# DeltaNet and MLP mixer on one core: the same steps in another global issue order

## The chip, the cores and the metric

The kernel runs on one core of one Trainium2 chip. Its time is the time on the device of one launch, in microseconds (us). The shares and durations come from a profile of one execution: TensorE is PE in it (its weight loads PEld), VectorE is DVE, ScalarE is ACT, GpSimd is POOL, and SyncE is SP, whose queue issues all the DMAs here.

## The reference, cut to what matters

```
# q, k, v: 4 batches x 8 heads x 768 steps x 48; beta: one weight per step
k_n = k / (norm(k) + 1e-6)
for t in range(768):                       # per batch and head, state is 48 x 48
    y[t] = q[t] @ state
    v_old = state.T @ k_n[t]
    state = state + beta[t] * outer(k_n[t], v[t] - v_old)
x = y, heads side by side                  # 4 x 768 x 384
h = relu(x.T @ w_tok1) @ w_tok2            # mixes the 768 tokens, through 256
u = x + h.T
out = u + relu(u @ w_ch1) @ w_ch2          # mixes the 384 channels, through 1536
```

All of it is computed in fp32. The MLP's weights arrive as 64-bit floats and are turned into fp32 words on the core.

## The kernel before

The recurrence is worked in chunks. A unit `u` is 128 steps of all 8 heads of one batch (24 units), and one recurrence step `t` is half a unit, 64 steps of the sequence (48 of them). Within a unit the dependence between its steps is a triangular matrix that is inverted; between units a 48 x 48 state is carried. The whole program is written as small jobs, each a Python generator that issues a few instructions and yields:

- `k{u}` (`load_kq`) loads k and q of a unit. From unit 12 on, the rows of k come first (calls 1 to 4, L363), then k in another arrangement, called kst (calls 5 to 8, L407), then the rows of q (calls 9 to 12, L363). `v{u}` (`load_v`) loads v in four DMAs (L407) and scales it on POOL (L416).
- `p{u}` (`prep`) squares kst on ACT (`ksq`, L442), makes the norms (L445 to L456), turns k and q (on PE, L466 and L484, for the first 12 units; with a transpose on DVE, L372, afterwards), multiplies them on PE (`p_g`, L504), masks on DVE (L510), and hands the blocks on: by copies (L569) for the first 6 units, by DMAs to DRAM (L577) for the others.
- `i{r}` (`invert`) inverts the triangles of a round of units on DVE (L613 to L641, in the main `sub` and `x`, L621 and L626). Rounds hold units 0-3, 4-5, 6-9, 10-13, and so on.
- `f{u}` (`from_parts`) brings the inverse back, by copies (L588) or DMAs (L593, `gm<-w_dram`); `h{u}` (`join_16`, L656 to L671) and `j{u}` (`join`, L685 to L718) complete the triangles from smaller ones.
- `r{t}` (`recur`) is the recurrence. PE computes `p_k` (L741), DVE `rest` (L746), PE `p_y` and `p_w` (L759, L763), ACT copies `w_t` (L767), PE computes `p_s` and the rest of `p_y` (L775, L776), DVE updates the state `s_t` (L785), ACT writes the result into `xb` (L790). The next step needs `s_t`.
- `m{b}` (`mixer`) is the MLP of batch b: token mixing (`p` L931, `p_h` L944), transposes (`p_ut` L954, copied to `u_t` L958), the first channel weight (batch 0: `p_c` L1011; the others: `p_r` L903, a scheme with 15 products of summed weights in place of 18), and the second (`p_o` L1033, seven products in place of eight). Its first six calls take one unit of the batch each as the recurrence writes it.
- `w{n}` turn the weights: a DMA (L271), two operations on ACT (L277, L278), one on DVE (L280), one on POOL (L285), one on DVE (L287). `s` (`sum_weights`) makes the sums of the first channel weight in 16 calls, one or two operations on DVE each (L842, L844). Six of these write into `lent`, the place of the k and q buffers of units up to 11, which have no other use afterwards; others overwrite blocks of the weight.
- `z`, `x` and `Y` (`keep_warm`, L225, and `warm_tiles`, L235) are fillers: matmuls of zeros into a PSUM tile that nobody reads.

No scheduler orders these at run time. A text at the end, `order`, names the job of which the next call is made, 2317 words with repeats (`p4*2` is two calls). All instructions are issued in that order; each engine, and SP's queue, executes its own in the order of issue, and waits for operands and buffers by semaphores:

```
for word in order.split():
    name, _, n = word.partition("*")
    for _ in range(int(n or 1)):
        next(jobs[name])
```

So the text decides for each engine what stands behind what. PSUM tiles come from four small sets: "prep" (2), "seq" (2, the recurrence), "mlp" (3) and the fillers' one.

Of the kernel before, what the change touches and what calls it, by code (L numbers as in the profile page):

```python
# [23 lines left out]
def kernel(  # L24
# [50 lines left out]
    NCB = DM // 128  # L75
# [182 lines left out]
    def piece_of(w, j, col):  # L258
        assert (id(w), j, col - col % WP) in rounded
        return w[:, j]  # L260
# [550 lines left out]
    }  # L811

    def sum_weights():
        for cb in range(NCB):
            for f in range(NHT):
                piece_of(wc1, cb, f * 128)
        a = {(j, k): w_block(j, k) for j in range(3) for k in range(NCB)}
        add, sub = ALU.add, ALU.subtract
        made = (
            ("w12", a[1, 2], a[0, 2], sub), ("w11", a[0, 1], "w12", add),  # L820
# [9 lines left out]
        for i, (out, x, y, op) in enumerate(made):  # L830
            j = {"w13": 0, "w9": 0, "w1": 0, "w6": 1, "w7": 2, "w15": 2}.get(out)
            assert j is None or used.issuperset(range(FT * j, FT * j + FT))
            outs = sums[out]
            n = WB // len(outs)
            for h, o in enumerate(outs):
                cut = slice(h * n, h * n + n)
                p, q = (
                    sums[z][0][:, cut] if isinstance(z, str) else z if z is None else z[:, cut]
                    for z in (x, y)
                )  # L840
                if p is None:
                    nc.vector.tensor_scalar_mul(o, q, -1.0)  # L842
                else:
                    nc.vector.tensor_tensor(out=o, in0=p, in1=q, op=op)  # L844
            if out not in [m[0] for m in made[i + 1 :]]:
                summed.add(out)
            yield
# [255 lines left out]
    jobs["z"] = keep_warm(4)  # L1103
    jobs["y"] = jobs["Y"] = warm_tiles()
    order = """
    z w10*5 b k1 k0 b k1*5 p1 k0*2 p1 w1 k0*3 p0*2 b p1 z p0*7 p1*2 k3 w1 w2 w1*2 p0 w3
    k2 k3 p0*2 w1 p0 p1 k2 w6 k3*2 p1 w2 k5 w3 p1*4 w2 w3 k2*2 k4*5 k2*2 p2 p1*2 w3
    k3*2 p0 p2 p3 p2 k4 p3 p2*4 w3 x p2*3 k6 p1 p3 p0*2 p2 p1 p2 v0 p2 w2 p1 w2 k5*4 p0
    p3*7 k7*5 z p4*2 w18 p1 p3*2 p2 p3 p2 z p4*2 p2 p3 p2 p3*2 w13 p3 p4*2 i0 k7 w18 p4
    i0*2 k6*4 k8 i0*3 v1*2 i0*7 p4*2 Y p4*2 w13 p4 i0 w13 i0 w18 z w18 i0 h0 p4 w6 p5*2  # L1110
    p4 i0 h1 w18 p5 h1 p6 k8*2 v0*3 f0*3 w13 f0 k8 w13 h0 w6 p6 h2 p5 h2 f1*3 k5 v1*2
    h0*2 p5 f1 h0 f2 h0*2 j0 k8 p5 w17 w6 z p5*2 p7 w8 f2 w17 k6 p6 w6 j0 h1 w17 w8 p7
    w17 z j0*2 h1 f2*2 h1 p4 j0 p6 w8*2 p4 h1*2 v0 p4 z w17 h2 r0 h2 r0 p5*2 r0 w14
    h2*3 w11 j1 w8 r0 Y w14*2 p5 v1 w11 Y p5 r1 k9 p5 r0 w11 j1*2 p5*2 h3 r1 p5 z j2 p6
    f3 r1*3 w14 w9 f3 h3 k8 p6 k9*4 p5 k9 i1 v2 j1 r1 z i1*2 w14 w9 i1 p6 r2*2 p8 v2 j1
    i1 w0 j2 i1*2 r1 i1 f3*2 r2 h3 r2*3 j2 p6 r3 w9 k10 h3*4 p6 w11*2 p6*2 r2 w0 r3*3
    w9 j3 v2*2 i1 w9 p7 w0 p6*2 w0 w5 r3 k10 j2*2 v2 r3 k10 r4 r3 v3 j3*2 p7*2 w0 p7
    w24 p7 k10*2 p6 p8*2 v3 r4 v3*2 p6 r4 j3 r4 p7 w16 j3 i1*2 p6 i1 p6 i1 r4 p7 r4*2
    w5 i1*2 p9 k11 p7 r5*2 w5*2 p7*2 r5*2 v4 p7*4 p9 r5*2 p7 w24 p8 r5 r6 w5 v3 r6 p9
    w16 p8*2 r6 i1 p8 h4*2 w16*2 h5 r6 h5 i1 p8*2 v4 w27 v4 r6 w16 r6*2 p8*2 f4*4 w27  # L1120
    w28 w24*2 p8*2 r7*2 k11 h4 v4 h4*4 w27 w24 w26 r7*2 w27*2 p8 p9*6 r7 w28 r7*2 w28
    w7 p9*2 p8 p9*2 p8*2 j4 p10 w28 j4 f5 w26 w28 f5 m0 f5*2 h5 x p9*4 w7 v4 w7*2 w29
    w7 j4 i2 h5 j4 h5 w26 w29 h5 w26*2 j4 v5 r8 w29*2 p10 r8 w15 h5 k12 r8 j5 r8 w15
    v5*3 w29 i2*3 w15*2 r8 j5 i2 w12 j5 v5 r8 r9 i2*2 k10 k11 m0 r8 r9*2 i2 w4 w15 i2
    w12 k11 k12*2 r9 k12 i2 r9 i2*3 w12 k11 i2 r9 w4 i2 r9 w4 m0 i2 w4 r10*2 j5 w12 w22
    p10*2 k12 p10 i2 w22 v6 m0 w4 j5 r10 i2 k12*6 w12 k12 r10*2 i2 r10*2 m0 r11 i2 w19
    i2 w22 z w22 w19*3 k11 w31 r11 p10 i2 v6 w22 i2 w21 w19 v6 r11 i2*5 v7 i2*2 v7*2 v6
    v7 p11 v6 i2 r11 i2 p10*4 w25 v7 r11 p10 r11 m0 w31 m0*2 f6*2 m0*2 f6 p11*2 p10
    f7*3 m0*2 w31*2 p10 w21 w31 m0*3 w25*3 f6 j6 f7 w21 p12 m0 j6*2 j7 m0 p12 w25*2 w23
    p12 f8 p12 w27 w25 j7*2 w27 w29 m0 f8*2 w20 p11*2 w21*2 w23*3 r12*2 p11 m0 j8 r12*2  # L1130
    p10*3 w20 r12 w23 w32 f9 w23 p10 j8*2 r13 f8 r13 w25 f9 w30 p11 m0 p11 p12 r13
    w20*2 r13*3 p11*2 f9 p11 k13*8 r14 w32 r13 w32*2 f9 p11*5 w20 p12*3 k13*2 p11 w32
    r14 k13 w30 w29 m0*4 r14*2 p12 v8*2 w30 k13 p12 r14 p13*3 w30 r14 w30 m0*2 w33
    p12*2 r15*2 v8 p13*3 w29 r14 m0*2 v8 r15 p13 r15 w33*2 m0*3 r15 k14*5 r15 p13 j9 v8
    p13*3 r16 w33*3 m0 w23 r16 k14*2 w33 m0 k14 r15 p12 w27 p12 w31 j9*2 p12 m0*2 r16*2
    p13*2 r16*3 w31*2 j9 r17 w33 p14*3 p13*2 i3 r17 m0 p14 v9 w23 p14 r17 m0 r17*3 i3
    m0 v9 k14*2 i3 m0 i3*3 m0*2 i3*3 m0 i3 m0*2 i3 j9 i3 k14*2 i3*4 p14 i3*3 v10 m0
    i3*3 k15*5 r17 i3 k15 m0 i3 v9 p14 v10 k15 r18 i3*6 k15 v9 k15 p14 v9 r18 i3*2
    m0*14 v10 k15 p15 k15*2 m0*2 r18 v10 f12 p14*2 f10*4 p14 r18*2 f11*2 p15 f11*2 p15
    r18 m0*3 p15 m0 r18 r19 p15 r19 k16*3 m0*3 r19*2 k16*2 j10*2 s f12*2 r19*3 k16*2  # L1140
    j11 m0 p15*2 k16 v10 k16*3 m0 p14 k16 j10 j11*2 r20*2 m0 s*2 m0 r20 p15*2 f13 r20*2
    p15 v11*5 r20*2 p16 p15 p14 p16 m0 r21 j12 r21 m0 p16*3 k17 r21 j12 p16*2 k17*3
    r21*4 k17*4 f13 f12 k17*2 j12 m0 r22 m0 r22*3 m0 p17 k17 f13 r22 s k17 v12*2 r22*2
    s*2 p16*4 p14*2 p17*2 p15 r23*2 p16 m0*2 r23 p16 p15 p17*4 r23 p15*2 p16 m0*2 p16
    m0 p17*3 r23 p17 m0 s*3 p17*3 s p17 m0*3 v12*2 j13*2 s*3 m0*3 i4*4 m0*2 v12 k18
    i4*2 j13 v14 r23 r24 v14 m0 r24*2 i4 m0 i4 k18*2 m0 k18*6 i4*2 v14 m0*2 i4 r24 i4
    f13 m0*2 v14 i4 p18*3 i4 m0 r25 i4 m0*2 k18 i4 p18 r25 i4*3 m1*3 r24 m1 v13 p18
    k19*7 m1*2 i4*6 k18 v13*2 r25 j13 r25*3 k19 i4 v13*2 i4 m1 k18 i4 r26 i4*4 m1*3 j13
    r25 p18*2 k19*4 f16 r26 p19 m1*3 f14 m1*3 f14 p19 r26*2 v14 f14*2 p19 f15 p18*2
    r26*2 f15 m1*5 f16 f15 r27 f16 m1 r27 p19 m1 p19 k20 p18 r26 p18 k20*7 r27*2 j14  # L1150
    m1*5 p19*2 k20*2 r27*3 k20 p19 k20 j14*2 j15 s*2 m1 j15*2 v15*3 r28*2 m1*2 j16
    r28*2 m1 p19 r28*3 p19 s f15 m1 p20 m1 r29 p18 p20 p19 r29 p20*3 p19 k21 p20 m1*2
    k21 m1*3 r29 p20 v15 k21*6 p18*2 k21*4 r29 m1*2 p19 v15 v16 m1 r29*2 p20*4 r29 m1*2
    f17 m1*3 p20*4 m1*4 j16 f17 p19 j16 r30*2 m1*3 p21 r30*2 m1 p21*2 r30*2 p18 r30 p21
    r31*2 m1 p21 r31*3 p21*2 v20 f17 p21 f16 p19 r31 m1 p21*7 k22 r32 m1*2 v16*2 m1*7
    v16 j17 m1*3 v16 i5 r31 k22*6 j17 r32 k22*2 v20 m1*3 k22 i5 v20 m1 i5*2 m1 j17 m1
    i5*2 r32 k22 r32 i5 p22 f17 i5 p22 m1*5 r32*2 p22 m1 i5 p22 r33*2 r32 m1 p22 j17*2
    r33*2 i5*2 p22 m1*4 k22 i5 p22 m1*6 k23 i5 m1*2 i5 r33*3 m1*8 i5 m1*2 v20 v17 m1*8
    v17 r34 v17 k23 v17*2 k23*2 m1 r34 m1*3 i5 k23*2 m1*4 k23*2 p22 r34 p22*2 r34*3 p23
    i5*2 m1*3 i5*2 k23 r35 r34 v20 r35 v18 m1*2 v18 p22 k23 v18 i5 p23 i5 m1 i5 m1*4 i5  # L1160
    m1*2 i5*3 m1*7 k23 m1 i5*3 m1*3 k23 p23 m1*2 v18 i5 p23 m1*2 i5 f20*2 f19 r35*2 m1
    p23*2 f18 m1*4 f19 f18 m1 p23*2 m1*3 f18 m1*4 v18 p22 r35*2 p22*2 f18 p22 p23 f19
    m1*3 p23 f19 j18 m1 p23*4 m1*2 j18 j19 m1*2 j18 j19*2 m1*2 r36 p23 i6*2 r36 f20 i6
    m1*2 r36*2 i6*4 m1*2 j20 r37 m2*3 r36 r37 f21 m2 r37*2 m2*2 r37 v19*2 i6*2 v19 i6*6
    f21 v19 f21 r37 i6*3 j20 i6 r38 m2 j21 v19 r38 m2 r37 i6 j20 i6*2 m2*3 r38 f20 j21
    r38*4 m2*2 r39*2 v21*2 m2*4 r39*2 j21 m2*2 f21 m2*6 r39*3 m2*2 v21 i6 r40 m2*2
    r40*3 i6*2 j21 m2 r40*2 j21 r40 m2*3 i6*3 r41*2 v21 i6 m2 i6*3 f22*3 m2*4 r41 v21
    r41 m2*4 r41 m2*5 r41*2 m2*3 r42*2 v22 f23*2 m2 j22 m2*6 f23 r42 j22 r42*3 j22 m2*6
    v22 m2 r43*2 r42 m2*8 f22 m2*9 r43 m2 j23 m2*2 r43*4 j23 r44 m2 j23 m2*3 f23 m2
    v22*3 r44*3 v23 m2*5 r44*2 m2*3 r44 m2*7 r45*2 j23 r45 m2*3 j23 r45*3 m2 v23 m2*2  # L1170
    v23*3 m2 r46 r45 m2*3 r46 m2*18 r46*2 m2*8 r46 m2*2 r46 m2*2 r46 r47*2 m2*3 r47*2
    m2*10 r47 m3 r47 m3*2 m2 m3*3 m2*4 m3*6 m2*3 m3 m2*2 m3 m2*6 m3*2 m2 m3*158
    """
    for word in order.split():
        name, _, n = word.partition("*")
# [34 lines left out]
```

## Time and profile before

| what | us |
|---|---|
| median of 3 runs (lowest, highest) | 660.11 (658.21, 660.59) |
| span of the profiled execution | 651.8 |
| PE busy, PE weight loads busy | 611.7 (94%), 530.3 (81%) |
| DVE busy | 455.3 (70%) |
| ACT busy | 268.7 (41%) |
| POOL busy | 102.1 (16%) |

The page gives the profiled execution's own time as its span, from the first to the last instruction; a run's time holds what lies around that as well, 8.3 us between this span and the median. The shares are means over stages that differ: the first 130 us hold the preparation of 12 units, the first inversions and the turning of the weights, and PE has idle time only there. Matmuls overlap, so a busy PE is not PE at its best. A PEclk below 1.00 in a window says that the clock granted to PE was throttled for part of it; two groups of the same matmuls can so have different durations.

### The profile page before, as it was taken

How to read it: one execution, taken by the hardware profiler on the slowest of the kernel's cores; microseconds unless marked ns; L12 is line 12 of the kernel's file. 1: busy time of each engine (PE TensorE's matmuls, PEld its weight loads, DVE VectorE, ACT ScalarE, POOL GpSimd, SP SyncE). 2: the span in 40 equal slices, each digit the busy share in tenths (PEclk: the TensorE clock that was granted, in tenths of full speed). 3: DMA queues.
4: the chain of work that ended last, by engine and by line, in shares of the span. 5: the costliest groups of instructions: out<-in, count | busy, mean ns of one | idle time of the engine just before them, and what ended most of it. 6: DMA issues, size and time to landing. Idle time of an engine off the chain costs nothing.

```text
span 651.8 us, 22212 instructions
## 1 busy us (share of the span) xinstructions
PE 611.7 (94%) x9482; PEld 530.3 (81%) x9482; DVE 455.3 (70%) x1160; ACT 268.7 (41%) x659; POOL 102.1 (16%) x121
## 2 busy tenths in 40 slices
PE   6659888799999999999999999999999999999998
PEld 4446776557889988977989999868999987999997
DVE  4897766897889966888886999577826352372643
ACT  7769677437541234223543414125425140232240
POOL 2337235223420102003111101000000000000000
PEclk9869777799999999999999999999999999999999
DMA  9766446655543344424345222200120000000000
GB/s 182 151 144 144 112 93 175 153 137 140 128 105 81 79 109 89 106 72 115 85 78 134 51 55 61 61 14 18 36 48 3 26 2 0 25 1 25 2 25 24
DMA packets 135778, 50.30 MB, mean 77 GB/s; under 512 B 114656, under 2 KB 130144, under 8 KB 135680
## 3 DMA queue, kind: packets, MB, share of 16 engines
q1 hardware_dynamic: 135680, 48.89, 33.0%
q8 instruction: 74, 1.21, 0.7%
q14 instruction: 24, 0.20, 0.1%
HBM read 39.42 MB, written 9.44 MB: 75 GB/s over the span
## 4 chain that ended last, share of the span: by engine, by line
PE 79%; ACT 8%; DVE 7%; DMA 4%; issue 2%; SPq 0%; POOL 0%; ACTq 0%; DVEq 0%; POOLq 0%
PE p_o L1033 25%; PE p_r L903 19%; PE p_c L1011 8%; PE p L931 4%; PE p_h L944 4%; PE p_k L741 4%; PE p_g L504 3%; PE p_y L759 3%; PE p_s L775 2%; DMA d<-in_moe_w_ch_dram 2%; DVE x L626 2%; PE p_z L699 1%; DVE sub L621 1%; PE p_w L763 1%; PE p_y L776 1%
## 5 line engine op out<-in xcount | busy, mean ns | idle before, releaser
L1033 PE MATMUL p_o<-wc,r 128*128 128x192 f32 x720 | 126.8, 330 | 0.6 <-ACT u_t L958 0.6
L1033 PEld LDWEIGHTS p_o<-wc,r 128*128 128x128 f32 x720 | 116.7, 190 | 3.1 <-ACT u_t L958 1.1
L915 DVE TENSOR_TENSOR r<-r,p_r 128x512 f32<-128x512 f32 x90 | 59.6, 683 | 44.1 <-PE p_r L903 43.6
L912 ACT COPY r<-p_r 128x512 f32<-128x512 f32 x54 | 31.5, 585 | 98.7 <-PE p_r L903 89.6
L962 DVE TENSOR_TENSOR xb<-xb,p_o 128x192 f32<-128x192 f32 x84 | 29.5, 351 | 59.9 <-PE p_o L1033 59.0
L626 DVE TENSOR_TENSOR x<-x,sub 128x84 f32<-128x84 f32 (+24 forms) x178 | 59.0, 331 | 6.1
L621 DVE TENSOR_TENSOR sub<-x 128x84 f32<-128x84 f32 (+24 forms) x178 | 58.3, 327 | 4.2 <-DMA x<-n_dram 0.5
L1033 PE MATMUL p_o<-wc,s 128*128 128x192 f32 x288 | 51.5, 330 | 0.3 <-DVE xb L962 0.3
L1011 PE MATMUL p_c<-u_t,wc 128*128 128x256 f32 x216 | 51.1, 387 | 0.6 <-ACT u_t L958 0.6
L416 POOL TENSOR_TENSOR v_st<-v_st,nrm 128x384 f32<-128x384 f32 x24 | 20.7, 862 | 183.5 <-DMA v_st<-in_v_dram 96.8
L1033 PEld LDWEIGHTS p_o<-wc,s 128*128 128x128 f32 x288 | 46.7, 190 | 1.3 <-DVE xb L962 0.6
L285 POOL TENSOR_TENSOR w_f<-w_f,d 128x384 uint32<-128x384 uint32 (+1 forms) x34 | 34.0, 1004 | 81.7 <-DVE w_f L280 49.7
L1011 PEld LDWEIGHTS p_c<-u_t,wc 128*128 128x128 f32 x216 | 39.7, 190 | 6.3 <-ACT u_t L958 0.9
L919 ACT ACTIVATE r<-r 128x512 f32<-128x512 f32 x54 | 33.7, 631 | 23.8 <-DVE r L915 23.4
L767 ACT COPY w_t<-p_w 128x192 f32<-128x192 f32 x48 | 15.2, 318 | 65.1 <-PE p_w L763 64.6
L790 ACT ACTIVATE xb<-p_y 64x192 f32<-64x192 f32 x96 | 31.1, 324 | 24.7 <-PE p_y L776 9.4
L504 PE MATMUL p_g<-kq 48*64 48x128 f32 (+1 forms) x704 | 28.6, 300 | 11.2 <-ACT kq L488 8.4
L903 PE MATMUL p_r<-u_t,wc 128*128 128x128 f32 x288 | 38.3, 276 | 0.0
L903 PE MATMUL p_r<-t_d,wc 128*128 128x128 f32 x288 | 38.0, 282 | 0.0
L476 POOL TENSOR_TENSOR mb<-mask_c,cs 128x512 f32<-128x512 f32 x20 | 21.4, 1071 | 101.2 <-DVE cs L456 56.4
L931 PE MATMUL p<-xb,w 128*128 128x384 f32 x96 | 36.2, 526 | 0.0
L903 PEld LDWEIGHTS p_r<-u_t,wc 128*128 128x128 f32 x288 | 35.4, 192 | 0.2
(171 smaller groups left out, 1215.1 us busy)
## 6 DMA issues: line engine op xcount, KB each, us to landing
d<-in_moe_w_ch_dram SPq DMA_DIRECT2D x24, 384.0 KB, 3.4
v_st<-in_v_dram SPq DMA_DIRECT2D x96, 48.0 KB, 2.6
out_dram<-xb SPq DMA_DIRECT2D x23, 192.0 KB, 1.9
kst<-in_k_dram SPq DMA_DIRECT2D x64, 48.0 KB, 2.5
n_dram<-gm SPq DMA_DIRECT2D x72, 32.0 KB, 1.7
pads<-in_k_dram SPq DMA_DIRECT2D x24, 96.0 KB, 2.6
pads<-in_q_dram SPq DMA_DIRECT2D x24, 96.0 KB, 2.4
gm<-w_dram SPq DMA_DIRECT2D x72, 32.0 KB, 2.1
```

Source lines behind the costliest of these rows:

```text
L285: nc.gpsimd.tensor_tensor(out=f, in0=f, in1=lo, op=ALU.add)
L504: nc.tensor.matmul(p_g[cc][PAR[i ^ cc], p], kqt[f, p, cc, 0], kqt[f, p, cc])
L621: nc.vector.tensor_tensor(out=tmp, in0=y[:, :, 0:s, s : s + 1].to_broadcast([n, k, s, w]), in1=y[:, :, s : s + 1, s + 1 : m].to_broadcast( ...
L626: nc.vector.tensor_tensor(out=y[:, :, 0:s, s + 1 : m], in0=y[:, :, 0:s, s + 1 : m], in1=tmp, op=ALU.add,)
L790: nc.scalar.mul(y[:, :, D * i : D * i + D], p_y[PAR[1 - i]], 1.0 if c else -1.0)
L903: nc.tensor.matmul(p[:, i], pieces[i // width][:, at : at + 128], f[f"u{n}"], start=first and i == 0, stop=True, skip_group_check=True,)
L912: nc.scalar.copy(o, p)
L915: nc.vector.tensor_tensor(out=o, in0=o, in1=p, op=ALU.add if sign > 0 else ALU.subtract)
L919: nc.scalar.activation(o, o, ACTF.Relu)
L931: nc.tensor.matmul(p_1[dh], piece_of(w1, c, 0)[:, dh * 128 : (dh + 1) * 128], xb[:, c], start=(c == 0), stop=(c == NCH - 1),)
L1011: nc.tensor.matmul(p_c[:, k], piece_of(wc1, cb, f * 128)[:, f * 128 : (f + 1) * 128], u_t[:, cb], start=(cb == 0), stop=(cb == NCB - 1),)
L1033: nc.tensor.matmul(p, a[:, m], wc2[:, m, j], start=(start and i == 0), stop=(i == NM - 1), skip_group_check=True,)
```

## The change

The text `order` is replaced by another one, of 2307 words with repeats. It holds the same calls of every job, but for the fillers: 3 calls of `z` in place of 11, and 1 of `Y` in place of 3. Within a job the calls keep their order. The places of most calls shift by a few words on their engine; some loads and sums shift by more. `sum_weights` no longer asks, before its first sum, that all pieces of the first channel weight be turned: each sum now asks that of the blocks that it reads, because in the new order the first sum stands ahead of the last pieces. This is a check made while the program is built, and issues no instruction.

```diff
     def sum_weights():
-        for cb in range(NCB):
-            for f in range(NHT):
-                piece_of(wc1, cb, f * 128)
-        a = {(j, k): w_block(j, k) for j in range(3) for k in range(NCB)}
+        a = {(j, k): (j, k) for j in range(3) for k in range(NCB)}
+
+        def block_of(j, k):
+            for f in range(FT * j, FT * j + FT):
+                piece_of(wc1, k, f * 128)
+            return w_block(j, k)
+
...
             assert j is None or used.issuperset(range(FT * j, FT * j + FT))
+            x, y = (block_of(*z) if isinstance(z, tuple) else z for z in (x, y))
...
     order = """
-    z w10*5 b k1 k0 b k1*5 p1 k0*2 p1 w1 k0*3 p0*2 b p1 z p0*7 p1*2 k3 w1 w2 w1*2 p0 w3
-    k2 k3 p0*2 w1 p0 p1 k2 w6 k3*2 p1 w2 k5 w3 p1*4 w2 w3 k2*2 k4*5 k2*2 p2 p1*2 w3
...
-    i3*3 k15*5 r17 i3 k15 m0 i3 v9 p14 v10 k15 r18 i3*6 k15 v9 k15 p14 v9 r18 i3*2
-    m0*14 v10 k15 p15 k15*2 m0*2 r18 v10 f12 p14*2 f10*4 p14 r18*2 f11*2 p15 f11*2 p15
...
+    k0 b k1 k0*4 k1*4 k0 k1 w10 b p1 z p1*2 b p0 w1 w3 p0 k2 w10 k2 p0 p1 w10 p0 w10 p1
+    k3 k2 p0*3 k2 p0*3 w10 v0 k3 k5 k2 k4 k3 p0*2 w2 k4 p1 p0 k4 p1 k3 p1 k2 k4 p2*2
...
+    v10*2 j9 i3 v10 p14 r17 m0 p14 m0*3 r17 i3 r17 k15 m0 v9 i3*5 k15*2 m0*2 i3 r18 k14
+    v10 i3 r18 i3 k15 i3 m0*2 k15 p14 i3 k15 m0 r17 p14 i3 m0 k15 i3*3 m0 k15 m0 i3*2
+    p15 k15 p14 k15 m0 r18 p14*2 r18*2 f13 r18 p15 m0 f10 f11 k15 r18 f11 m0 f10 k15
...
     """
```

## The prediction

> **What bounds the kernel now.** I read the windows first, cut where the busiest engine changes. The page gives a span of 651.8 us; the median run is 660.11 us, so 8.3 us lie around the span. I sum on the span and add 8.3 at the end. A measurement of this kernel can tell about 0.5%, 3.3 us, from no change.
>
> ```profile
> core 0: us, PE busy (x) PEld busy (x) DVE busy (x) ACT busy (x) POOL busy (x), PEclk, DMA share, GB/s
> 4.20:30.00 25.80, 18.80 (x232) 14.39 (x232) 18.08 (x44) 23.00 (x62) 6.85 (x9) 0.93 1.00 164
> 30.00:42.00 12.00, 4.10 (x65) 2.50 (x67) 11.07 (x37) 3.99 (x9) 2.52 (x5) 0.70 0.74 156
> 42.00:72.00 30.00, 25.97 (x955) 19.44 (x947) 23.73 (x56) 27.56 (x73) 17.06 (x20) 0.83 0.57 134
> ```
> ```profile
> 72.00:90.00 18.00, 15.81 (x364) 14.21 (x368) 9.74 (x31) 8.99 (x29) 5.08 (x7) 0.53 0.46 105
> 90.00:124.00 34.00, 26.96 (x778) 20.74 (x781) 25.10 (x63) 23.13 (x60) 15.39 (x16) 0.75 0.63 161
> 124.00:200.00 76.00, 71.63 (x1261) 56.47 (x1253) 64.33 (x172) 38.08 (x101) 24.44 (x25) 1.00 0.49 118
> 200.00:400.00 200.00, 198.47 (x3074) 176.43 (x3073) 165.90 (x418) 69.20 (x175) 25.74 (x29) 1.00 0.38 89
> 400.00:635.00 235.00, 234.32 (x2711) 212.61 (x2711) 129.28 (x323) 72.51 (x152) 3.42 (x4) 1.00 0.09 21
> ```
>
> ACT carries 4 to 30 us (23.00 of 25.80) and 42 to 72 (27.56 of 30), DVE carries 30 to 42 (11.07 of 12), PE at half clock 72 to 90. From 124 us the clock is 1.00 and PE has its whole time from 200 on. There is nothing to win behind 200 us: PE idles 2.2 us between 200 and 635. Two things can move the end: the moment at which PE is full, and new holes behind it. The chain of waits agrees, and gives the rates of full work: 0.168 us a matmul for p_o, 0.114 for p_r, 0.219 for p_c.
>
> ```profile
> 608.91 12.07 PE p_o L1033 x72
> 592.35 13.66 PE p_r L903 x120
> 204.16 13.15 PE p_c L1011 x60
> ```
>
> **What the orders differ in.** Both hold the same steps, except for fillers: z falls from 11 to 3 and Y from 3 to 1. For every step I summed the durations that its instructions have in the trace, engine by engine, over all steps ahead of it in each order. Of the real PE work ahead, the new order has as much, within 1 us, at most steps of the recurrence (r1, r2, r3, r5, r10, r11). It is a local reshuffle, so the terms are small.
>
> **Start.** The load of w10 no longer leads. The k load of chunk 0 is issued where w10's was (0.74 us, against 1.65 for the first k load before), a gain of 0.9 at most; but w10's two roundings on ACT, which ran from 4.26 to 5.25 ahead of the first k data (5.98), now lie in ACT's full stretch: 1.0. I take 0, from -0.9 to +1.0.
>
> **To r3.** Ahead of h0's first step the new order has 4.0 us more DVE and 4.1 us more ACT work; ahead of r0's first step 1.5 and 1.6 us less. So the inversion that DVE carries alone ends later, and ACT's idle time beside it (8 of 12 us) is used. Ahead of r3 it is +0.6 DVE and +1.9 ACT; ACT being the full engine there, I take +1.0, from -1.7 (r0's figure) to +4.0 (h0's).
>
> **Fillers and the clock.** Six of the removed or moved fillers stood in 52 to 72, where the clock was 1.00; one Y and one z remain near there. First their PE time, then two groups at either clock (columns: busy us, mean ns, idle before):
>
> ```profile
> 52.00:72.00 20.00, 4.50 (x8) 1.19 (x8) 1.00 0.55 129
> 52.00:72.00 20.00, 1.23 (x16) 0.89 (x16) 1.00 0.55 129
> ```
> ```profile
> L504 PE MATMUL p_g<-kq 64*64 64x128 f32 x32 | 1.5, 275 | 0.0
> L741 PE MATMUL p_k<-s_t,wc 48*64 48x48 f32 x48 | 2.0, 220 | 0.0
> ...
> L504 PE MATMUL p_g<-kq 64*64 64x128 f32 x64 | 4.3, 422 | 1.4 <-ACT xb L790 1.4
> L741 PE MATMUL p_k<-s_t,kq 48*64 48x48 f32 x32 | 2.2, 307 | 0.5 <-DVE s_t L785 0.5
> ```
>
> PE's 17.70 us in 52 to 72 hold 5.73 of fillers, so 12.0 of work. At half clock p_g grows from 1.5 to 2.15 per 32 and p_k from 0.67 to 1.1 per 16, about 1.5 times: 18.0 us, plus 1.8 for the two fillers. In 72 to 90, without fillers, PE was busy 88% of the time. 18.0 at 88% is 20.5 us (+0.5), 19.8 is 22.5 (+2.5). If the clock stays full, PE needs 13.8 us and ACT, with 18.22 us of work in that window, sets the pace: -1.8. I take 0 with those ends, since ACT covers PE either way within half a microsecond. The z at 134 us (1.2 us at full clock) goes from a stretch where PE is 94% busy: -1.1.
>
> The stretch from 72 to 90 shows that small matmuls at 88% busy did not bring the clock up. The Trainium skill (TensorE: Matmul & The Clock Gate, "Part 1: The HAM clock gate") says instead that about 3.4 us of sustained activity releases the clock and an idle window throttles it again. By that rule 72 to 90 should have run at full clock, and the fillers were not needed; the trace does not agree (0.53).
>
> **Links without cover.** Where p_w's group is followed directly by p_s's of the same step, PE waits for ACT's w_t about 0.5 us. Eight steps up to r16 stand so before (r1, r3, r5, r8, r9, r10, r13, r16), two after (r8, r10); behind them it is r30 and r31 before and r30 after. In the stretch where it matters that is -3.0 at most. Other PE work between p_w and p_s, and shorter covers at p_z, p_g and h, give back 1.8 or more by the same count over all links (shortages of 12.3 us before, 14.1 after). I take -0.6, from -3.0 to +1.8.
>
> **Moved sums.** The first sum (L844, 0.65 us on DVE at 229 us before) now stands between r11 and m0's dense part, the next two (0.69 each) near r15. DVE has 11.7 us idle in 124 to 200 and covers them; uncovered they cost 2.0. What sum 1 reads and overwrites is finished by then (chunk 10's k turns stand 117 steps ahead), so nothing waits behind it on DVE. I take 0.
>
> **Loads nearer to their use.** This is the largest difference from r12 on. PE work between the last kst load of a chunk and the ACT square (L442) that reads it averages 7.7 us before (chunks 12 to 23, 2.1 at least) and 1.6 after (0.0 at least). The kst row lands in 2.5 us, the gm row in 2.1.
>
> ```profile
> kst<-in_k_dram SPq DMA_DIRECT2D x64, 48.0 KB, 2.5
> ...
> gm<-w_dram SPq DMA_DIRECT2D x72, 32.0 KB, 2.1
> ```
> ```profile
> 273.62 0.52 ACT L442 ACTIVATE ksq<-kst 128x384 f32<-128x384 f32 x1 [2.91 <-DMA kst<-in_k_dram]
> ```
>
> Nine chunks fall short of 2.5 us, by 13.0 us in all (0.4 before). Between f and j, where DVE's transpose L685 reads gm, five fall short of 2.1 by 7.1 us (none before). For the q loads and L372, against 2.3 us, it is 4.0 (2.3 before). Together 21.4 us more of ACT and DVE standing at a load: the upper end. Queued behind the square on ACT are the copies of w_t, for which PE's p_s waits; behind L685 on DVE are the updates of s_t and the evictions of p_o and p_r. The lower end is 0: SP runs its queue by its own waits, not by the steps beside it, and in the two places before where ACT stood at the square (2.91 us above, 3.67 at 296 us) PE lost nothing. The nearest row is that one. I take +1.5, the price of the one place, chunk 16, where a w_t copy comes within 1.0 us of PE work behind the square (short by 1.9).
>
> **Sum.** +1.0 - 1.1 - 0.6 + 1.5 = +0.8: span 652.6 us, time 660.9, no change that can be told.
>
> **Rivals.**
> *Faster: PE has fewer holes and the clock holds.* -3.0 (links) - 1.8 (52 to 72 at ACT's pace) - 1.1 (the z at 134) = -5.9: 654.2 us. For it: the direct links are fewer, and m0's first step, with full 128-row matmuls, comes about 100 steps earlier (beside i1). Against it: 0.53 in 72 to 90 without fillers. The Trainium skill's rule on the clock (same page and section) would put the time here.
>
> *Slower: the loads arrive late.* One mechanism, at ksq (L442) and t11 (L685): if SP is no more than 2.5 us ahead of PE from 180 to 480 us, DVE, 83% busy from 200 to 400, passes on its 8.8 us (7.1 at gm, 1.7 more at q), and ACT at least chunks 15 and 16 (1.2 + 1.9). With the +0.3 of the other terms (1.0 + 0 - 1.1 - 0.6 + 1.0 for the start) that is +12.2: 672.3; with half of it, 666. For it: the covers above. Against it: PE idled 1.5 us in 200 to 400 in spite of both waits, and spreading the loads frees SP's queue, which before issued four kst loads in 2.58 us in a row, behind v loads that wait for DVE.
>
> *The clock falls and ACT doesn't cover:* +2.5, or 663.4, the edge of no change; it is in the middle case.
>
> **How the numbers follow.** No change 0.36, faster 0.31, slower 0.33. The middle case is the likeliest, but each side has one mechanism that I can price and not exclude. Range: 650 (the faster rival and the better ends of the start and of r3) to 672 (the slower rival in full); the middle case alone spans 657 to 664.
>
> **What the new profile would show.** If the sum holds: real PE work full from about 124 us, the window 200 to 400 at 198 us busy or more, ksq waits of 1 to 3 us with no PE wait for w_t beside them. If the slower rival: PE waits for w_t or s_t, or p_o evictions late, of several us behind 180 us, and DMA named as releaser for L685 and L442. If the faster: the clock at 1.00 in most of 50 to 90, and r11 several us before 137. I am wrong altogether if the window 42 to 72 grows or shrinks by over 5 us, since equal ACT work stands ahead in both.

## The result: 3.6% slower

| | before | after |
|---|---|---|
| median (lowest to highest), us | 659.16 (655.29 to 660.59), 4 runs | 681.46 (678.93 to 683.16), 4 runs |
| span of the profiled execution, us | 651.8 | 681.4 |
| PE's holes behind 150 us | 4.1 | 16.8 |

The ratio is 1.0364, 95% interval 1.0305 to 1.0423, forecast 660.9 in a range up to 672. "Holes" are all the time behind 150 us in which the trace has PE on no matmul. An execution of after takes 1.8 us more than its span (683.16 against 681.4). So the profiled execution of before took 653.6 us and lies near the lower end of its runs, which go from 650 to 663 us; the two profiles differ by 29.6 us where the medians differ by 22.3.

The windows of after, cut as in the prediction (columns as there):

```profile
core 0: us, PE busy (x) PEld busy (x) DVE busy (x) ACT busy (x) POOL busy (x), PEclk, DMA share, GB/s
4.20:30.00 25.80, 17.14 (x216) 13.42 (x217) 18.29 (x42) 22.37 (x60) 5.78 (x8) 0.93 1.01 163
30.00:42.00 12.00, 4.17 (x43) 3.19 (x41) 11.18 (x32) 6.66 (x16) 3.45 (x5) 0.63 0.58 136
42.00:72.00 30.00, 20.11 (x718) 16.59 (x718) 21.23 (x42) 20.22 (x52) 17.12 (x20) 0.50 0.48 116
72.00:90.00 18.00, 17.58 (x520) 15.47 (x514) 14.42 (x43) 12.56 (x38) 4.29 (x6) 0.66 0.52 112
90.00:124.00 34.00, 27.42 (x796) 23.16 (x789) 22.87 (x59) 21.82 (x59) 14.41 (x15) 0.72 0.65 149
124.00:200.00 76.00, 67.54 (x1160) 50.50 (x1158) 68.27 (x155) 37.76 (x96) 25.18 (x25) 0.90 0.51 123
200.00:400.00 200.00, 188.37 (x2913) 164.05 (x2911) 150.76 (x375) 64.21 (x167) 25.08 (x27) 0.98 0.38 84
400.00:635.00 235.00, 233.13 (x2823) 211.30 (x2822) 137.63 (x357) 72.03 (x156) 6.76 (x8) 1.00 0.12 27
```

Two stretches have changed. In 42 to 72 ACT falls from 27.56 to 20.22 of 30 us, and PE from 955 matmuls to 718 at clock 0.50. In 200 to 400, where PE had missed 1.5 us, it now misses 11.6; DVE and ACT have become less busy too, so nobody took over the work. The chain that ended last, which was 79% PE before, says the same in one line:

```profile
PE 45%; DVE 14%; SPq 6%; DMA 6%; issue 2%; ACT 1%; POOL 0%; DVEq 0%; POOLq 0%; ACTq 0%
```

To see where the time goes, I take the first instruction on DVE, ACT or POOL of some calls (i0:2 is the second call of `i0`), in us, for these profiles and for some of the kernels described below:

| profile | i0:2 | r1:2 | r3:2 | r8:2 | r10:2 | r17:2 | r36:2 | span |
|---|---|---|---|---|---|---|---|---|
| before | 31.8 | 61.8 | 71.4 | 112.6 | 129.2 | 190.9 | 414.5 | 651.8 |
| after | 33.8 | 66.8 | 81.1 | 113.9 | 135.7 | 206.0 | 448.2 | 681.4 |
| e1 (old head, new tail) | 31.7 | 61.6 | 70.8 | 112.9 | 129.1 | 199.4 | 436.2 | 669.6 |
| e2 (new head, old tail) | 34.0 | 66.8 | 77.7 | 111.4 | 133.2 | 197.7 | 420.9 | 657.9 |
| e9 (e1, transfers by due time) | 31.8 | 65.6 | 74.7 | 118.6 | 134.4 | 207.7 | 449.4 | 682.5 |
| e13 (e1, 132 loads left out) | 31.8 | 61.8 | 71.4 | 113.4 | 129.6 | 197.0 | 423.8 | 656.7 |

After loses 9.7 us up to r3, has them back but for 1.3 at r8, is 15.1 late at r17 and 33.7 at r36. From r36 to the end it needs 233.2 us where before needs 237.3: 4 us of work stand earlier. PE's holes behind 150 us are 12.7 us more, 11.6 of them between r17 and r36. That stretch is 18.6 us longer, and these holes, those 4 us and a stretch at half clock (below) make up about as much.

**What the holes are.** The waits of after between 150 and 480 us (us in total, times, longest), and below them those of before for x and for kst; before has no row for gm or the q rows. In before DVE waits for transfers 2.5 us in all in this stretch.

```profile
DVE t L685 <- DMA gm<-w_dram: 5.9, 4, 1.7
DVE sub L621 <- DMA x<-n_dram: 4.6, 3, 3.3
DVE kq L372 <- DMA pads<-in_q_dram: 4.0, 3, 1.8
...
ACT ksq L442 <- DMA kst<-in_k_dram: 23.8, 8, 5.2
...
PE p_s L775 <- ACT w_t L767: 3.3, 3, 1.8
PE p_z L699 <- DVE t L685: 2.5, 2, 1.5
PE p_g L504 <- DVE kq L372: 2.1, 2, 1.9
PE p_x L702 <- DMA gm<-w_dram: 1.9, 2, 1.0
```
```profile
DVE sub L621 <- DMA x<-n_dram: 0.5, 2, 0.3
...
ACT ksq L442 <- DMA kst<-in_k_dram: 6.6, 2, 3.7
```

One of them, followed through: SP's queue, then DVE, then PE, in after's timeline (start, duration, instruction, idle before it and releaser).

```profile
269.84 0.55 SPq L363 DMA_DIRECT2D pads<-in_q_dram  x1
270.43 1.54 SPq L577 DMA_DIRECT2D n_dram<-gm  x1
272.02 0.93 SPq L363 DMA_DIRECT2D pads<-in_q_dram  x2
273.04 0.87 SPq L577 DMA_DIRECT2D n_dram<-gm  x2
273.95 0.45 SPq L593 DMA_DIRECT2D gm<-w_dram  x1
274.45 0.94 SPq L577 DMA_DIRECT2D n_dram<-gm  x2
275.43 0.45 SPq L363 DMA_DIRECT2D pads<-in_q_dram  x1
...
277.71 1.08 DVE L372 STREAM_TRANSPOSE kq<-pads 128x512 f32<-128x512 f32 x1 [1.81 <-DMA pads<-in_q_dram]
...
278.85 0.67 PE L504 MATMUL p_g<-kq 48*64 48x128 f32 x16 [1.85 <-DVE kq L372]
```

The place of these four q rows was free at 265.8, when `p16` had turned its own. SP issues back to back, half a microsecond for each transfer, and the last row comes out at 275.43, behind five transfers to DRAM and a gm row that is wanted at 283.8 only. It lands at 277.7; DVE and then PE wait 1.8 us for it. The transfers of kst and gm themselves are no slower than before (2.5 and 2.1 us there). The q rows' median is 3.3 us in after, where it was 2.4, and 2.5 in e1, which has such waits too; so a slower transfer may have part in after's waits, but is not needed for them:

```profile
kst<-in_k_dram SPq DMA_DIRECT2D x64, 48.0 KB, 2.6
...
gm<-w_dram SPq DMA_DIRECT2D x72, 32.0 KB, 2.0
```

The Trainium skill (DMA: Bandwidth & Descriptors, "Issuing engines are not separate DMA queues") says that the time in which a sequencer initiates a DMA "is usually small relative to the DMA itself". Here it is 0.43 to 0.61 us beside 2.0 to 2.6 us of landing, but one queue issues them all, in order. A unit's 24 transfers (12 for k and q, 4 for v, 4 to DRAM and 4 back) make some 12 us of turns.

**The clock behind the holes.** In before's profile the granted clock is 1.00 from 124 us to the end of PE's work. In after's it is at half in two stretches behind 142 us, the second one right behind the hole of 1.8 us at 252 (after, cut there):

```profile
142.20:152.50 10.30, 9.02 (x89) 6.38 (x89) 9.65 (x29) 2.84 (x8) 1.93 (x2) 0.50 0.61 156
254.90:261.70 6.80, 6.80 (x84) 6.27 (x74) 2.49 (x8) 1.04 (x5) 0.83 (x1) 0.50 0.21 42
```

A matmul takes up to twice as long there (p_g took about 1.5 times in the prediction's rows), so these 17.1 us lose up to 8.5 us beside the holes; that is an estimate. Behind 150 us the profile of e1, described below, has holes as long in sum as after's and a clock of 1.00. Those of e9 and e20 are at half clock for 17 us, that of e5 for 27, that of e11 for 37, and in these four such a stretch begins in every hole of 3 us or more, before the hole ends. Holes of 1.8 to 2.3 us have it in some places (after at 252) and not in others (after at 277, e1 at 266). So a long hole costs more than its length.

**The head.** Here one transfer holds up the others. SP's queue in after:

```profile
34.80 0.59 SPq L407 DMA_DIRECT2D v_st<-in_v_dram  x1
50.03 0.33 SPq L271 DMA_DIRECT2D d<-in_moe_w_tok_dram  x1
```

w8's load needs the buffer of w6, whose last step on DVE (L287) stands behind the first inversion. SP stands in front of it for 15 us, with the loads of k7, k8 and v1 behind it. Before, those loads stood ahead of any load that waits for such a buffer.

### The profile page after: what moved, and what is told of

It is laid out like the page before. It is cut to its first block, busy times and chain, and to the rows that moved or that the text cites. A ratio compares the mean times of both kernels' runs of the same rounds, so it can differ in the third digit from the quotient of the medians.

```text
span 681.4 us, 22150 instructions
## 1 busy us (share of the span) xinstructions
PE 618.3 (91%) x9450; PEld 539.4 (79%) x9450; DVE 468.7 (69%) x1160; ACT 268.7 (39%) x659; POOL 103.7 (15%) x121
## 4 chain that ended last, share of the span: by engine, by line
PE 45%; DVE 14%; SPq 6%; DMA 6%; issue 2%; ACT 1%; POOL 0%; DVEq 0%; POOLq 0%; ACTq 0%
PE p_o L1037 16%; PE p_r L907 15%; DVE sub L621 3%; DVE x L626 3%; PE p L935 2%; PE p_h L948 2%; SPq L407 2%; SPq L577 2%; PE p_c L1015 1%; SPq L593 1%; PE p_k L741 1%; DVE kq L372 1%; PE p_y L759 1%; SPq L363 1%; DMA kst<-in_k_dram 1%
## 5 line engine op out<-in xcount | busy, mean ns | idle before, releaser
L1037 PE MATMUL p_o<-wc,r 128*128 128x192 f32 x720 | 129.2, 333 | 0.6 <-ACT u_t L962 0.6
L1037 PEld LDWEIGHTS p_o<-wc,r 128*128 128x128 f32 x720 | 118.6, 192 | 4.1 <-ACT u_t L962 1.1
L626 DVE TENSOR_TENSOR x<-x,sub 128x84 f32<-128x84 f32 (+24 forms) x178 | 64.8, 364 | 6.1
L621 DVE TENSOR_TENSOR sub<-x 128x84 f32<-128x84 f32 (+24 forms) x178 | 61.5, 346 | 7.7 <-DMA x<-n_dram 4.6
L923 ACT ACTIVATE r<-r 128x512 f32<-128x512 f32 x54 | 33.8, 631 | 31.6 <-DVE r L919 31.3
L1015 PEld LDWEIGHTS p_c<-u_t,wc 128*128 128x128 f32 x216 | 39.6, 190 | 6.1 <-DVE xb L966 0.5
L504 PE MATMUL p_g<-kq 48*64 48x128 f32 (+1 forms) x704 | 31.3, 319 | 14.4 <-ACT kq L488 12.1
L935 PE MATMUL p<-xb,w 128*128 128x384 f32 x96 | 39.3, 553 | 0.8 <-ACT xb L790 0.8
L504 PEld LDWEIGHTS p_g<-kq 48*64 48x64 f32 (+1 forms) x704 | 25.2, 160 | 15.9 <-ACT kq L488 12.8
```

The lines of the kernel that those rows point to most:

```text
L504: nc.tensor.matmul(p_g[cc][PAR[i ^ cc], p], kqt[f, p, cc, 0], kqt[f, p, cc])
L621: nc.vector.tensor_tensor(out=tmp, in0=y[:, :, 0:s, s : s + 1].to_broadcast([n, k, s, w]), in1=y[:, :, s : s + 1, s + 1 : m].to_broadcast( ...
L626: nc.vector.tensor_tensor(out=y[:, :, 0:s, s + 1 : m], in0=y[:, :, 0:s, s + 1 : m], in1=tmp, op=ALU.add,)
L923: nc.scalar.activation(o, o, ACTF.Relu)
L935: nc.tensor.matmul(p_1[dh], piece_of(w1, c, 0)[:, dh * 128 : (dh + 1) * 128], xb[:, c], start=(c == 0), stop=(c == NCH - 1),)
L1015: nc.tensor.matmul(p_c[:, k], piece_of(wc1, cb, f * 128)[:, f * 128 : (f + 1) * 128], u_t[:, cb], start=(cb == 0), stop=(cb == NCB - 1),)
```

## The experiments

An order is cut here at m0:8, at about 145 us: head and tail. "Old" is the order of before, "new" that of after. Ratios are against before on the same chip, with 95% intervals; 1% is 6.6 us, so that the change as a whole, at 3.64%, counts as 24 us.

**e1 and e2: which half.**

```diff
 e1:  order up to m0:8
-new
+old
      order behind it: new
 e2:  order up to m0:8: new
      order behind it
-new
+old
```

> Calls up to and with the mixer's eighth for batch 0 (about 142 us in the old profile) in the old order, all later ones in the new. In the two profiles that call stands 10.7 us later with the new order, and the end 29.6 us later. If the calls behind it cost 19 us by themselves (loads that arrive late at ACT and DVE): 678. If what they cost comes from how the head left the queues (SP late, clock low), the tail costs under 5 us here: 660 to 665.

> The other way round: the new order up to the mixer's eighth call for batch 0, the old one behind it. If the tail's order is what costs 19 us: 671 (the 10.7 us of the head remain). If the head's lateness makes the tail's holes: 680. If the head's lateness is made good later because PE is full anyway: 660 to 665.

Measured: e1 669.66 us, 1.0182 (1.0107 to 1.0257); e2 660.18 us, 1.0058 (1.0024 to 1.0092). The tail alone costs 12 us, between the two expectations; the head alone costs 4, as the third expectation has it. 8 of the 24 come only of both together, give or take 7 by the three intervals. PE's holes behind 150 us are 17.2 in e1 and 4.9 in e2.

**e3 and e4: the fillers.**

```diff
 e3: new order
-6 fillers, in the new places
+16 fillers, each behind the same PE call as in the old order
 e4: old order
-16 fillers
+6 fillers, each behind the same PE call as in the new order
```

> The new order with all fillers of the old one (11 z, 2 x, 3 Y), each behind the PE call that it stood behind there. If the half clock from 33 to 84 us is what makes the head late: the clock is 1.00 from about 52 to 72 us again, and 8 to 10 us come back, 671 to 673. If ACT and SP set the pace there: no more than 3 us, 678 or more.

> The old order with the new one's fillers alone (3 z, 2 x, 1 Y). If the fillers are what the head lost: 668 to 670. If ACT covers PE in that stretch, as the prediction had it: 658 to 662.

Measured: e3 678.32 us, 1.0314 (1.0248 to 1.0379); e4 655.10 us, 0.9983 (0.9946 to 1.0019). The old kernel loses nothing without ten of its fillers; with them the new one comes back by some 3 us, which the intervals (after: 1.0305 to 1.0423) don't separate from none. So e3 came as its second expectation has it, and e4 is below both of its own.

**e5 and e7: the transfers as early as their buffers allow.**

```diff
 e5: order of e1;  e7: new order
-loads of k, v, x, stores and loads of gm (e7: the weights' too): as they stand
+the same in SP's old relative order as far as that goes, each as soon as its buffer's last user stands ahead of it
```

> The order that e1 has (old up to m0:8, new behind it) for everything that computes, stores or adds; only the calls of the tail that issue nothing but DMAs (k, v, x, the stores and loads of gm) stand in the old relative order of SP's queue, each as soon as its buffer is free. Theory L (the tail's loss is loads that stand nearer to their use: the engine that takes them waits in order, DVE sub<-x 6.7 us, kq<-pads 6.6 us, t<-gm 5.9 us, ACT ksq<-kst 22.5 us in e1, and PE's holes behind 150 us grow from 4.1 to 17.2 us): the holes close and the time falls from e1's 669.7 to 655-661 us. Theory C (the loss is the order in which DVE's and ACT's steps stand to PE's, whatever the loads do): 667-671 us, PE's holes stay near 17 us. A time between says how much each has.

> The new order for everything that computes, stores or adds, through the whole kernel; all calls that issue nothing but loads (the weights' too) and the stores and loads of gm stand in the old relative order of SP's queue, each as soon as its buffer is free, 70 of them where their user stands. L: the tail's 12-13 us come back and so does the part of the head that hangs on SP's stand from 34.8 to 50.0 us; 656-664 us. C: 675-682 us. If the head's compute order costs by itself what e2 showed (4 us) and the loads the rest: 660-664.

Measured: e5 685.3 us, 1.0466 (1.0389 to 1.0544); e7 724.29 us, 1.1049 (1.097 to 1.1128). Both miss every expectation, by far and upwards. A load that stands right behind its buffer's last user makes SP wait for that user, and all that is queued behind waits too. In e5 it is the weights' loads: ACT stands at them, the copy of `u_t` behind them in ACT's queue is late, and PE has one hole of 8.2 us, with half clock from 152 to 162 us behind it:

```profile
ACT d L277 <- DMA d<-in_moe_w_ch_dram: 23.6, 7, 9.9
...
PE p_c L1015 <- ACT u_t L962: 8.2, 1, 8.2
```

So these two do not tell the theories apart, but they show that the places in SP's queue alone move this kernel by 19 us (e5 against e1) and 45 us (e7 against after): nothing that computes has changed places.

**e8: SP's stand in the head.** In the new order, seven loads move up:

```diff
-... p6 h0 w8 w18 k8 f1 ... w18 w17 j0 h0 k6 h1 ... w17 j0 k7 v1 w17 ... k8 w17 r0 ... k7 h1 k7 ...
+... p6 h0 k8 k6 k7 v1 k8 k7*2 w8 w18 f1 ... w18 w17 j0 h0 h1 ... w17 j0 w17 ... w17 r0 ... h1 ...
```

> The new order; only seven loads of k6, k7, k8 and v1 (calls k8:1, k6:6, k7:4, v1:4, k8:2, k7:5, k7:6) are moved up ahead of w8's load, which is the call that SP stood at from 34.8 to 50.0 us. Theory S (that stand delays the steps that follow and is what costs the new head its 4 us and the two halves together some 8 us more): 668-674 us, with DMA traffic in 42-52 us again near 100 GB/s and m0:8 earlier by several us. Rival (the stand is hidden, the head loses by the order of its computing): 677-682 us, PE's first steps of p7 and r3 where they were.

Measured: 674.66 us, 1.0299 (1.0235 to 1.0362). Some 4 us come back, a little less than theory S expected; the interval overlaps that of after.

**e9 and e10: the transfers by due time.**

```diff
 e9: order of e1;  e10: order of e8
-SP's queue from 160 us on, as it stands
+at every turn, of the transfers whose buffer or data is free in the trace, the one needed first
```

> The order of e1 (old up to m0:8, new behind it); only SP's queue between 160 and 440 us stands in another order: of the transfers whose buffer or data was free in e1's trace, the one that is needed first goes first (272 of 307 change places, by 6 on the mean). Nothing that computes or stores to the output changes places. Theory L (the tail's 12-13 us are transfers that were issued too late although their buffer had long been free, such as k13:12, free at 170.6, issued at 178.3, used 2.6 us later; DVE waits 20 us for ten of them between 150 and 480): DVE's waits for those transfers fall under 6 us, PE's holes behind 150 us from 17.2 to 4-8 us, the time from 669.7 to 656-662. Theory C (the order of the computing steps on DVE and ACT against PE is the loss): the waits go but the time stays at 666-671, PE's holes near 17 us.

> The order of e8 (the new one with seven loads ahead of w8's), with SP's queue between 160 and 450 us by due time as in e9. L: 674.7 falls by about 12 to 660-665, and what is left above the 656-659 of before is the head's. C: 672-677.

Measured: e9 679.79 us, 1.0372 (1.0297 to 1.0446); e10 675.89 us, 1.0313 (1.0248 to 1.0378). e9 misses both expectations; e10 lies where theory C (the order of the computing steps) had it, but holds no test of it, since e9 shows other transfers late. Of e9's small holes most are gone, but there are four large ones (1.7 to 4.7 us), three of them with half clock behind: what had been put off until due now came too late as a group, x behind thirteen rows to DRAM (DVE waits 5.4 and 6.1 us for x) and k20's kst behind 21 other transfers, issued back to back from 326 us on.

**e11: the old computing, the new distance of loads to use.**

```diff
 old order, behind m0:8
-loads of k, q and x, stores and loads of gm: as they stand
+each as many calls ahead of its user as in the new order
```

> The old order of everything that computes; behind m0:8 the loads of k and q, the stores and loads of gm and the loads of x stand as many calls ahead of their user as they do in the new order (251 of them, in the new order's turn; v's loads and the weights' stay). L: the old kernel gets the tail's loss from its loads alone, 664-672 us, with waits of DVE for x, the q rows and gm of 10-20 us in 150-480. C: 655-660, as before.

Measured: 688.06 us, 1.0492 (1.043 to 1.0553). It is far slower than before with no computing step moved, as theory L says, but by 32 us in place of 8 to 16, so it is no copy of the new tail's loss. The holes are 24.6 us, and the clock is at half for 37 us behind 150.

**e12 to e14: fewer transfers.** The three orders (old, e1's, new), each without the 132 loads of k's and q's rows from unit 13 on; the kernel leaves them out and computes these units with the rows of earlier ones, so only its time is of use:

```diff
-                nc.sync.dma_start(
-                    out=rows_of[i][r : r + HB, :, 0 : G * D - f], in_=rows[par, :, :, f:]
-                )
+                if u < TU + 1:
+                    nc.sync.dma_start(
+                        out=rows_of[i][r : r + HB, :, 0 : G * D - f],
+                        in_=rows[par, :, :, f:],
+                    )
...
-                nc.sync.dma_start(
-                    out=dst[PAR[par ^ cc], :, cc], in_=rows[par, cc]
-                )
+                if src is v or u < TU + 1:
+                    nc.sync.dma_start(
+                        out=dst[PAR[par ^ cc], :, cc], in_=rows[par, cc]
+                    )
```

> The old order without the loads of k's and q's rows from unit 13 on: the kernel leaves out 132 of the DMAs (12 for each of 11 units) and computes those units with the rows of the units before. All steps that compute, store or load anything else stay. It is the measure for e13 and e14. All theories: 650-657 us, since PE has hardly a hole behind 150 us in the old order.

> The order of e1 (old up to m0:8, new behind it) with the same 132 loads left out. Theory L (the tail's 12-13 us come of transfers that SP's queue gives out too late: in e1 it issues them back to back at 0.43 to 0.61 us each while DVE and ACT wait in 17 places): with nearly half of the queue's work gone the waits go, and the time comes within 4 us of e12. Theory C (the order of the computing steps against one another): still 9-13 us above e12.

> The new order throughout with the same 132 loads left out. L: 4-9 us above e12 (the head's loss stays). C: 17-23 us above e12, as much as the whole loss.

Measured: e12 655.5 us, 1.0017 (0.998 to 1.0054); e13 657.44 us, 1.0037 (1.0 to 1.0073); e14 664.56 us, 1.0149 (1.007 to 1.0228). The tail's loss falls from 12 us to 1 (e13 against e12), with the order of computing untouched; theory C asked for 9 to 13 us above e12. The windows of 200 to 400 us, in the order e1, e13:

```profile
200.00:400.00 200.00, 188.65 (x2895) 165.21 (x2896) 155.41 (x390) 64.49 (x168) 24.87 (x27) 1.00 0.37 82
```
```profile
200.00:400.00 200.00, 198.84 (x3115) 175.86 (x3113) 165.25 (x417) 69.37 (x179) 26.14 (x29) 1.00 0.19 44
```

And DVE's waits for transfers and ACT's for kst in 150 to 480, e1 and then e13, whose lines stand 3 later in the file and which has no row for kst:

```profile
DVE sub L621 <- DMA x<-n_dram: 6.7, 3, 4.0
DVE kq L372 <- DMA pads<-in_q_dram: 6.6, 3, 3.3
DVE t L685 <- DMA gm<-w_dram: 5.9, 5, 2.3
...
ACT ksq L442 <- DMA kst<-in_k_dram: 22.5, 7, 7.4
```
```profile
DVE t L688 <- DMA gm<-w_dram: 2.2, 3, 1.1
DVE sub L624 <- DMA x<-n_dram: 1.9, 1, 1.9
```

The waits for x and gm fall from 12.6 to 4.1 us although these transfers are still there: they come out sooner, and SP has fewer turns to give. The rest went because the k and q rows that DVE and ACT had waited for were themselves left out, so e13 does not say how much the turns alone are worth. Of after's 24 us, 14 go in the same way (e14). The 9 that stay above e12 are not late k or q rows.

**e15 and e16: SP's stand once more.** The seven loads of e8 moved up, in e14 (e15) and in e2 (e16); the edits are those.

> The order of e8 (new, with seven loads moved ahead of w8's) with the 132 loads of k's and q's rows from unit 13 on left out as in e14. If SP's stand from 34.8 to 50.0 us is what the head loses: 657-660 us, within 3 us of e13's 657.4. If the head loses by the order of its computing: 663-666, as e14.

> The order of e2 (new up to m0:8, old behind it) with the same seven loads ahead of w8's; nothing is left out. If SP's stand is the head's loss: 654-658 us, where e2 took 660.2 (1.0058 of before). If it is not: 659-661.

Measured: e15 661.03 us, 1.0087 (1.0055 to 1.0119); e16 659.85 us, 1.0069 (1.0041 to 1.0096). With the new tail the stand is worth about 4 us again (e14 to e15, as after to e8), between the two expectations; with the old tail nothing (e2: 1.0058).

**e18 and e19: where the head loses.**

```diff
 e18: order up to i0:17;   e19: order up to r8:2
-old
+new
      order behind it: old
```

> The new order up to the first inversion's last step (i0:17), the old order behind it; nothing is left out. Every profile of a new head has i0:2 some 2.0 us and r1 some 3-5 us later than those of an old head. If that shift stays to the end: 658-661 us (1.005 or more of before). If it is made up behind (r8:2 is as early with the new head as with the old): 654-657.

> The new order up to the recurrence's step r8:2, the old order behind it. If the head loses in its first 110 us: 658-662, as e2's 660.2. If it loses between r8 and m0:8 (r10:2 is 1-6 us later with the new head, r8:2 is not): 654-657.

Measured: e18 657.9 us, 1.0058 (1.0029 to 1.0088); e19 662.78 us, 1.0152 (1.0104 to 1.0201). The start up to the first inversion already costs what the whole new head costs in e2. (The profiled execution of e18, with a span of 652.5 us, doesn't show where that stays.) e19 is slower than both and than its expectations, though its order is e2's up to r8 (108.5 us in its profile): a seam between two orders has a price of its own. e1 and e2 have one seam each, so their shares are good to a few us.

**e20: the same transfers from another queue.**

```diff
-                nc.sync.dma_start(
+                queue = nc.sync if src is v or u < TU + 1 else nc.gpsimd
+                queue.dma_start(
                     out=dst[PAR[par ^ cc], :, cc], in_=rows[par, cc]
                 )
```

The rows of k and q (L363) are issued likewise.

> The order of e1 (old up to m0:8, new behind it) with nothing left out, but the 132 loads of k's and q's rows from unit 13 on, which e13 left out, are issued from POOL's queue and not from SP's; every call keeps its place. POOL is busy 8 to 13 of 50 us there. If what e13 gave back (12 us) is the turn in SP's one queue: 657-663 us. If POOL, which also executes in order, stands in front of loads whose buffer isn't free, and passes that on to the masks that it makes for p_g, or issues each load more slowly than SP: 668-685. If it is the transfers themselves (DMA engines, DRAM) and not the queue: 667-671.

Measured: 676.77 us, 1.0333 (1.0266 to 1.04). POOL's own work is in order too. By its profile it waits 23 us for a v row ahead of a k load, and the masks and scalings behind come late:

```profile
POOL v_st L419 <- DMA v_st<-in_v_dram: 69.1, 6, 37.9
POOL pads L364 <- DMA v_st<-in_v_dram: 23.4, 1, 23.4
```

So this is the second of its expectations, and it leaves open what the first asked: whether the transfers would be in time from a queue that has nothing else to wait for. What speaks for the queue and against the transfers is only read from profiles: their landing times are about the same in before and e1 (kst 2.5 and 2.6 us, gm 2.1 and 2.0, q rows 2.4 and 2.5), and the DMA engines are 0.37 to 0.38 busy in 200 to 400 in before, e1 and after. Part of what e20 loses against e1 can be the clock, at half for 17 us behind 150 where e1's is full.

## Why the prediction was wrong

**The step that failed: loads nearer to their use.** This term was put at +1.5 us. It counted the right waits. Nine chunks were to fall short at the square; eight ACT waits are there, 23.8 us. L685 was to have 7.1 us; it has 5.9. The q rows were to have 1.7 more than before; it is 4.0. The upper end was 21.4 us more of ACT and DVE standing; 27.1 came (17.2 at the square, 5.9 and 4.0). But then it priced them by "the nearest row", two waits of ACT at the square in before in which PE lost nothing, and took 1.5, for the one place where a copy of w_t comes close behind a square. Those rows were of ACT. In before DVE hardly waits for a transfer behind 150 us, so no row said what such a wait is worth, and DVE is the engine that hands PE s_t, t, kq and the evictions. PE's holes behind 150 us grew by 12.7, and PE's longest rows of waits there beside w_t name t, kq and gm, as shown above. That DVE's waits, and not ACT's, make the holes is read from these rows; no run takes one without the other. The argument for the lower end, that "SP runs its queue by its own waits, not by the steps beside it", is what misled: by its waits and by its turns. Half a microsecond each, in order, was in the profile of before (four kst loads in 2.58 us) and was not summed. The x rows, 4.6 us in after and 6.7 in e1, were not counted at all. Without the loads of k and q the tail's loss falls by 11 us (e13) and the whole one by 14 (e14): so much did these loads alone cost, where the term had 1.5 for all of them.

**The slower rival** named this mechanism and its place, DVE and ACT at L685, L442 and the q rows, with PE waits behind 180 us, and priced it at +12.2. The tail alone cost 12 (e1), 11 of which went without the k and q loads (e13). That 12.2 and 12 meet so closely is partly luck: the rival left out the x rows and the clock, and counted two of the ACT waits only. It had a third of the chance and set the top of the range, 672; what lay beyond is the head, which it took at +0.3.

**Start.** Taken as 0, from -0.9 to +1.0. The profiles with the new head have i0:2 at 33.5 to 34.5 us (but e7, whose loads stand elsewhere: 45.0), those with the old one at 31.4 to 32.4. The step weighed who loads first (k0's copies on ACT do come 3.7 us earlier, k1's 0.2) and not DVE: in after a weight's last step (L287, 1.11 us) and a reduction (L445, 0.54 us) stand right ahead of the transpose that opens the inversion. e18 gives the start 0.6% by itself, 4 us where 1.0 was the end.

**To r3.** Taken as +1.0, from -1.7 to +4.0, out of sums of work ahead. From i0:2 on, r3 is 7.7 us later (47.3 us after i0:2 where it was 39.6). Sums of work see no engine that is made to stand, and here SP did, 15 us in front of a buffer. But the stand is a small part of it: from i0:2 to r3 the other profiles with this whole head (e7 aside) need 43.5 to 45.7 us with the stand and 42.4 to 43.7 without (e8, e10, e15, e16), those with the old head 39.1 to 42.9. After's own is the longest, with half clock from 33 to 84 us. The text called itself wrong altogether if 42 to 72 moved by over 5 us; it did. What the stand costs in the end is smaller and depends on what follows: 4 us with the new tail, none with the old (e8, e15, e16).

**Fillers and the clock.** 0 was right for the fillers (e4: 0.9983). The ends, -1.8 and +2.5, were too near for the clock. e1 and e9 have the same order up to 160 us and differ at r10:2 by 5.3 us. The windows of 52 to 72, e1 and then e9:

```profile
52.00:72.00 20.00, 16.88 (x608) 12.36 (x607) 15.02 (x42) 18.61 (x51) 11.52 (x14) 1.00 0.58 131
```
```profile
52.00:72.00 20.00, 18.82 (x530) 13.55 (x526) 11.62 (x29) 15.31 (x40) 10.15 (x13) 0.72 0.47 107
```

The clock rose at 49.6 us in e1 and at 63.0 in e9, and PE needed more time for fewer matmuls. That differs from execution to execution of one order; the profile of before, at 1.00 in this window, was no measure of what the new order would meet. Chance is not all of it: with the new head up to r8 or further the half clock that every profile has at 46 us lasts until 63.6 to 84.2 us, with the old head and its fillers until 49.6 to 51.9, but for e9, and in e4, without ten fillers, until 62.0. In e4 this later rise costs nothing in the end. The Trainium skill (TensorE: Matmul & The Clock Gate, "Part 1: The HAM clock gate") says that the window in which activity is watched runs freely, so that the same kernel warms up differently from run to run. e1 and e9 agree with that. Its figure of under 1% of a span is for the ramp when a kernel starts; the 5.3 us here, 0.8%, come of a later rise, so no run tests it.

**The z at 134 us** (-1.1) is below what a run here tells; e4, without it and nine others, is 1.1 us faster by its ratio, with no change inside the interval.

**Links without cover** was taken as -0.6, from -3.0 to +1.8. PE's waits of whole runs for w_t went from 4.8 to 5.1 us and for s_t from 4.0 to 6.6, a sum of +2.9, beyond the worse end. That count sees only what stands between two PE groups; the longest wait for w_t, 1.8 us at 252, is in the stretch of late transfers, and the clock falls to half behind it.

**Moved sums** were taken as 0, uncovered 2.0. In e1 two of them (0.68 and 1.32 us) stand directly ahead of the update of s_t at 183.65, and PE waits 1.0 us for it. No run isolates them.

**The 8.3 us around the span** were not there: 1.8 are, and 6.5 were the scatter of before.

**The other two rivals.** The faster one asked for the clock at 1.00 in most of 50 to 90; it was 0.50 until 84 us. That the clock falls without cover (+2.5) did come so in after's profile, but e4 shows no cost of it that the fillers decide, and no run isolates the rest.

What was right: nothing was won behind 200, the fillers cost nothing, and the mechanism and place of the slower rival. That PE idles next to nothing behind 200 in before did not say that nothing could be lost there: the new holes and the half clock behind one of them came in just that stretch.

**What stays open.** Of the 24 us, by ratios, the tail alone has 12 and the head alone 4; 8 appear only when both stand together. SP's stand has about 4 of these (after to e8, e14 to e15), each time with intervals that overlap; the other 4 no run separates. Behind 150 us after's profile has 9.3 us at half clock, at most 4.7 us of time by estimate, and e1's and e2's have none, so the clock can be a part of the 8. That SP's turns, and not the number of transfers as such, make the tail's loss rests on the chain shown above and on the waits for x and gm that shrink in e13, where the loads left out were also among those waited for; e20 was to show it and did not.

## What to carry to other kernels

When an issue order changes, treat the DMA queue as an engine: sum its turns between the moment when a buffer is free and the moment of use, and look for every load that waits for a buffer, because all behind it wait too, so "earlier" can be as bad as "later" (e5, e7). Price a new wait by the engine that will stand, not by the nearest wait of another engine: here DVE, 83% busy from 200 to 400 us in before, seems to have handed its waits on. Count the clock behind a long hole as well. And take what lies around the span from an execution whose time and span are both known.

## What the runs showed of the hardware

With no computing step moved, e9 and e5 take 12 and 19 us more than e1 by their ratios, and e11 takes 32 us more than before: that much hangs on the order of one queue that issues a transfer each 0.43 to 0.61 us, and on the clock, which falls to half in PE's holes of 3 us or more in these three. The clock granted to PE rises up to 13 us apart in two executions of the same order, worth 5 us at r10.
